# A second-pass down-projection by seven products, LayerNorm tiles turned by DMA, and moved modulation sums

## The chip, the cores and the metric

The kernel runs on one core of one Trainium2 chip. The metric is the device time of one execution in microseconds. The engines are named as in the profile: PE (TensorE matmul), PEld (its weight loads), DVE (VectorE), ACT (ScalarE), POOL (GpSimd), SP (SyncE, which issues most transfers).

## What is computed

The reference is one block: adaptive LayerNorm, attention over a cache, and a gated feed-forward part. x is 2048 x 512, there are 32 query heads of 128 over the last 512 cached keys, and the inner width F is 1792.

```python
mod = (_silu(c) @ w_mod).reshape(c.shape[0], 6, 1, -1)
sa, ca, ga, sb, cb, gb = (mod[:, 0], mod[:, 1], mod[:, 2], mod[:, 3], mod[:, 4], mod[:, 5])
h = _layernorm(x, axis=-1) * (1 + ca) + sa
x = x + ga * _A_ref(h, A_k_cache, A_v_cache, A_wq, A_wo)
h = _layernorm(x, axis=-1) * (1 + cb) + sb
x = x + gb * _B_ref(h, B_w_gate, B_w_up, B_w_down)   # (gelu(h @ w_gate) * (h @ w_up)) @ w_down
```

## The kernel before, in words

**Arithmetic.** Each f32 operand is split into two f16 halves, a high and a low one ("pair"), and a product is three f16 matmuls (`mm3`, lines 85 to 88: low x high, high x low, high x high). A matmul has 128 rows of contraction, a 128 x 128 stationary tile and 512 moving columns.

**Stages.** First the modulation vectors and the first LayerNorm; then attention in 512 steps t of one 128-row score tile each (`scores`, `peak`, `expo`, `recips`, `high`, `low`); then the feed-forward part. Attention runs in two halves of 1024 rows (t up to 255, and from 256). The rows' running sum lies in eight tiles `acc`. When a half's last head is done, `attn_final` stores the tile; in the first half it also normalises it for the feed-forward part (`ln_tile` with gen 2), in the second it only keeps the statistics (`ln_last`).

**Feed-forward.** Rows are taken in two passes of 1024 (two blocks of 512, qb 0 and 1), F in seven pairs of 128-wide tiles. n = 0 to 13 counts pairs over both passes; a round q = 2n + m computes the gate (m = 0) or the up-projection (m = 1) of a pair for both row blocks. Each round uses Strassen's scheme in its seven-product form on blocks of 2 x 2: products 1 to 7 (`PROD`, `CHAIN`, order in `ORDER`) of six matmuls each. They build up in three PSUM banks: chain `a` (products 1, 6, 7, 4; ACT copies the partial sum out after 1, 6 and 7: `keep`, L847), `b` (2) and `c` (5, 3). DVE adds the copies and banks (L1232); ACT and DVE apply the gelu (L1239, L1242, L1245, L1249); in m = 1 DVE multiplies gate and up (L1260), ACT makes the f16 high part (L1262) and DVE the low part (L1263). The results are the four tiles A["11"], A["21"], A["12"], A["22"]: columns of the pair by block of rows.

**Down-projection.** `y_tasks` multiplies A with two 128 x 512 tiles of w_down (`WO["f", n, 0 or 1]`): per pair eight row tiles of two groups of three matmuls, each with its own bank `py`, and DVE adds the bank to `acc` (L914). The eight tasks of a pair wait in `nexty`; `y_next` takes one after each of four of the seven products of a round, so that PE has something between products of one chain.

**What sets the order.** In attention the order on every engine is written out by hand (`tc.manual_schedule`, positions t in `at`, `sched`). In the feed-forward part a planner orders the engines' instructions by program order and readiness, with its own estimate of times; only SP keeps the order in which its transfers are written, and a transfer that waits holds up all behind it. `f_at(q, k, ...)` hangs work on the place behind the k-th product of round q; a "step" is 7q + k.

**Other work around the change.** Gate and up weights come as pairs from DRAM (`set_fetch`, on SP), the combined input blocks of the second pass ("gen 3") are made in the first: `ln_tile(3, i)` loads a row tile, normalises it on ACT (L487), turns it with four f32 transposes on PE (L495, bank `pln`), applies scale and shift on ACT in four 128-wide passes (L503), and spills it; `combos(3, p)` reads the spilled tiles back into `raw` buffers and makes differences on POOL (L540, L367). Tile pools limit how much is in flight: `raw` 5 buffers, `rw` 2, `p16` 4, `pt` 3, PSUM `acc` 5 banks, `s` 2, `qa` 1. The modulation sums for shift and scale (j = 3, 4) are eight products with a running sum on DVE (`mod_col`, L135) at steps t = 211 to 229 of attention; `mod_scale` at t = 234 scales them.

Of the kernel before, what the change touches and what calls it, by code (L numbers as in the profile page):

```python
# [10 lines left out]
F32 = mybir.dt.float32  # L11
# [6 lines left out]
P = 128  # L18
# [45 lines left out]
def block_kernel(ctx: ExitStack, tc: tile.TileContext, x, kT, v, wq, wo, wg, wu, wd, cT, wc, wm, out):  # L64
# [248 lines left out]

    def store(key, t, slack=6):
# [150 lines left out]
    def ln_tile(gen, i, src):  # L465
# [11 lines left out]
        def stat():  # L477
            ln_stat(st["x"], st)
            ln_power(st)
            if gen == 2:  # L480
                st["nm"] = small.tile([P, 1], F32, name="nmean")
                pool_ts(st["nm"], st["mv"][:, 0:1], st["rs"], -1.0)

        def norm():
            if gen == 3:
                rs, nm = col("kmax", qb * QT + i), col("kinv", qb * QT + i)
                return nc.scalar.activation(st["x"], st["x"], AF.Identity, bias=nm, scale=rs)  # L487
            if gen == 2:
                return nc.scalar.activation(st["x"], st["x"], AF.Identity, bias=st["nm"], scale=st["rs"])
            nc.vector.tensor_scalar(st["x"], st["x"], st["mv"][:, 0:1], st["rs"], op0=ALU.subtract, op1=ALU.mult)  # L490
# [6 lines left out]
        def affine(dts):  # L497
# [7 lines left out]
            if KT - 1 in dts:  # L505
                def spill():
                    dma(spilled(gen, qb)[:, :, i * P:(i + 1) * P], f.rearrange("p (k q) -> p k q", k=KT))

                if gen == 3:
                    put_off(3, spill)  # L510
                else:
                    spill()

# [10 lines left out]

        more = [lambda: parts(True), lambda: parts(False)] if gen < 3 else []
        return load, [nop if gen == 3 else stat, norm, turn, lambda: affine((0, 1)), lambda: affine((2, 3))] + more

# [308 lines left out]
    def banks(st, tags):  # L836
        def bk(k):
            def get():
                if k not in st:
                    st[k] = bank(*tags[k])  # L840
                return st[k]
            return get
        return bk
# [289 lines left out]
    at(("w", 232), lambda: mx.update(m=mod_max(3)))  # L1133
    at(234, lambda: mod_scale(3, "mf", 1.0, mx["m"]))

# [79 lines left out]
    NQ = 4 * NP  # L1215
    B, A, G = {}, {}, {}

# [8 lines left out]
    def f_items(q, hold=None):  # L1226
# [27 lines left out]
        def result(key, src):  # L1254
# [3 lines left out]
            else:  # L1258
                g = G.pop((n, key))
                nc.vector.scalar_tensor_tensor(g, g, 0.5 * GU, src, op0=ALU.mult, op1=ALU.mult)  # L1260
                t = pair("ot", "at", NOT)
                nc.scalar.activation(t[:, 0, :], g, AF.Copy)  # L1262
                nc.vector.tensor_tensor(t[:, 1, :], g, t[:, 0, :], op=ALU.subtract)  # L1263
                A[n, key] = t

# [27 lines left out]

        tags = {"a": ("s", "fa", 2) if q else ("qa", "fa", 1), "b": ("acc", "fb", NACC), "c": ("acc", "fc", NACC)}
        return with_posts(("f", q), 2 + q // (2 * NP), banks(st, tags), after)

    def f_spread_at(q):
# [224 lines left out]


    def y_next():
        if nexty:
            all_of(nexty.pop(0))
    ORDER = (1, 2, 6, 7, 5, 4, 3)

    def f_at(q, k, *fns):
        at(("f", q, k), *fns)  # L1530

    for n in range(1, 2 * NP):
        for k in range(2):
            f_at(2 * n + 1, 2 * k, lambda n=n, k=k: WO.update({("f", n, k): fetch(("wd", n % NP, k), get_wo())}))
    for q in range(3, NQ):
        for k, at_ in ((0, 2), (3, 2), (1, 3), (2, 4)):
            f_at(q - 1, at_, lambda q=q, k=k: set_fetch(("f", q), ("f", q % (2 * NP)), k))

    for i in range(2 * QT):
        load, steps = ln_tile(3, i, lambda i=i: y1[2 * QT + i])  # L1540
        q = 7 * (2 + i // 2) + 3 * (i % 2)
        f_at((q - 4) // 7, (q - 4) % 7, load)
        for k, fn in zip((0, 2, 4, 5, 6), steps):
            f_at((q + k) // 7, (q + k) % 7, fn)
    for p in range(2):
        q = 7 * (7 + 2 * p)
        for load, steps in combos(3, p, nc.gpsimd):
            f_at((q - 2) // 7, (q - 2) % 7, load)
            for off, fn in steps:
                f_at((q + 2 * off) // 7, (q + 2 * off) % 7, fn)  # L1550

# [8 lines left out]
    for q in range(NQ):  # L1560
        n, m = divmod(q, 2)
        its = items(NG + q) if q < 2 else f_items(q)
        for k, pk in enumerate(ORDER):
# [11 lines left out]
    while nexty:  # L1575
        y_next()
    while waits_:
        tick()
# [35 lines left out]
```

## Time and profile before

| what | us |
|---|---|
| three runs | 1769.34, 1772.45, 1772.27; median 1772.27 |
| the profiled execution | 1769.1 |
| its span | 1767.3 |
| PE busy | 1730.0 (98%) |
| DVE busy | 1447.2 (82%) |
| ACT busy | 1219.3 (69%) |
| POOL busy | 882.2 (50%) |

The feed-forward part begins at about 1345 us of the span. A group's row reads: line, engine, operation, output <- inputs, shapes, count, then busy time in all and the mean of one in ns, then the idle time of the engine just before and what ended it. A window's row reads: stretch, length, then busy time of PE, PEld, DVE, ACT and POOL with counts, granted PE clock, DMA share, GB/s. A row of waits reads: who waited for whom, us in all, times, longest.

### The profile page before, as it was taken

The page shows a single profiled execution, that of the slowest core. Times are in us where ns is not written, and L with a number is a line of the kernel's source. Part 1 is how long each engine was busy: PE and PEld are TensorE (multiplying, and loading weights), DVE is VectorE, ACT ScalarE, POOL GpSimd, SP SyncE. Part 2 cuts the span into 40 slices and gives each one's busy share as a digit, 9 for nine tenths or more (in the row PEclk, how much of TensorE's full clock was granted, in tenths as well). Part 3 has the DMA queues.
Part 4 walks back from the last instruction along what each step waited for, and adds up shares of the span by engine and source line. Part 5 has one row for each costly group of instructions (what it writes and reads, how often), then busy time and mean ns, then how long its engine had stood idle before and what let it go on. Part 6 is the DMA issues. An engine that isn't in the chain of part 4 may idle for free.

```text
span 1767.3 us, 25992 instructions
## 1 busy us (share of the span) xinstructions
PE 1730.0 (98%) x8114; PEld 796.3 (45%) x8114; DVE 1447.2 (82%) x2501; ACT 1219.3 (69%) x2830; POOL 882.2 (50%) x1119
## 2 busy tenths in 40 slices
PE   7899999999999999999999999999999999999998
PEld 4444444444444444444444444444444444444443
DVE  7888888888888998888888888888886768767676
ACT  5887787878778777897777777777674555434342
POOL 4879878776788873444565555555520024000000
PEclk9999999999999999999999999999999999999999
DMA  7999999989999997999999999999985643252222
GB/s 230 209 195 210 218 217 200 223 204 221 216 216 227 224 201 145 208 205 234 208 208 208 212 214 204 206 211 214 188 185 131 199 129 114 83 173 90 86 75 75
DMA packets 662122, 327.62 MB, mean 185 GB/s; under 512 B 553056, under 2 KB 575840, under 8 KB 661984
## 3 DMA queue, kind: packets, MB, share of 16 engines
q1 hardware_dynamic: 661696, 325.44, 80.0%
q8 instruction: 64, 1.05, 0.3%
q14 instruction: 74, 0.61, 0.1%
q10 hardware_dynamic: 288, 0.52, 0.1%
HBM read 131.73 MB, written 59.90 MB: 108 GB/s over the span
## 4 chain that ended last, share of the span: by engine, by line
PE 72%; DVE 14%; ACT 8%; issue 3%; POOL 2%; DMA 1%; SPq 0%; ACTq 0%; POOLq 0%; DVEq 0%
PE py L86 7%; PE py L88 7%; PE py L87 7%; DVE p L971 5%; PE ps L86 4%; PE ps L88 4%; PE ps L87 4%; PE po L86 4%; PE po L88 4%; PE po L87 4%; DVE nm L945 3%; PE fa L86 3%; PE fa L88 3%; PE fa L87 3%; ACT ee L954 2%
## 5 line engine op out<-in xcount | busy, mean ns | idle before, releaser
L954 ACT ACTIVATE ee<-ps,nm 128x512 f32<-128x512 f32 x512 | 350.9, 685 | 251.0 <-DVE nm L945 245.6
L971 DVE SCALAR_TENSOR_TENSOR p<-ee,rr,p 128x512 f16<-128x512 f32 x512 | 470.0, 918 | 0.9 <-ACT p L966 0.7
L945 DVE TENSOR_REDUCE nm<-ps 128x1 f32<-128x512 f32 x512 | 349.4, 683 | 77.0 <-PE ps L88 75.5
L966 ACT ACTIVATE p<-ee,rr 128x512 f16<-128x512 f32 x512 | 365.4, 714 | 2.3 <-DMA pt<-p 1.9
L86 PE MATMUL ps<-k,qt 128*128 128x512 f16 x512 | 194.1, 379 | 16.6 <-DVE qt L706 15.4
L86 PE MATMUL py<-wo,ot 128*128 128x512 f16 x512 | 194.1, 379 | 4.4 <-DVE ot L706 4.4
L87 PE MATMUL po<-pt,v 128*128 128x512 f16 x512 | 194.0, 379 | 0.0
L88 PE MATMUL po<-pt,v 128*128 128x512 f16 x512 | 194.0, 379 | 0.0
L87 PE MATMUL py<-wo,ot 128*128 128x512 f16 x512 | 194.0, 379 | 0.0
L88 PE MATMUL py<-wo,ot 128*128 128x512 f16 x512 | 194.0, 379 | 0.0
L86 PE MATMUL po<-pt,v 128*128 128x512 f16 x512 | 194.0, 379 | 0.0
L88 PE MATMUL ps<-k,qt 128*128 128x512 f16 x512 | 194.0, 379 | 0.0
L87 PE MATMUL ps<-k,qt 128*128 128x512 f16 x512 | 193.9, 379 | 0.0
L962 DVE RECIPROCAL rr<-rr 128x2 f32<-128x2 f32 x256 | 41.4, 162 | 99.6 <-ACT rr L959 98.5
L87 PEld LDWEIGHTS <-w 128*128 128x128 f16 x728 | 71.2, 98 | 86.2 <-issue 1.2
L88 PEld LDWEIGHTS <-w 128*128 128x128 f16 x728 | 71.2, 98 | 86.0 <-issue 0.2
L86 PEld LDWEIGHTS <-w 128*128 128x128 f16 x728 | 71.2, 98 | 85.5 <-DVE w L1016 0.3
L914 DVE SCALAR_TENSOR_TENSOR acc<-py,dysc,acc 128x512 f32<-128x512 f32 x112 | 81.6, 747 | 31.5 <-PE py L88 30.5
L954 ACT ACTIVATION_READ_ACCUMULATOR ee<-ps,nm 128x1 f32 x512 | 100.8, 197 | 0.0
L914 DVE SCALAR_TENSOR_TENSOR acc<-py,ysc,acc 128x512 f32<-128x512 f32 x128 | 94.7, 740 | 3.9 <-PE py L88 3.9
L706 DVE SCALAR_TENSOR_TENSOR ot<-po,ot 128x512 f16<-128x512 f32 x128 | 87.0, 680 | 0.0
L86 PE MATMUL py<-wo,at 128*128 128x512 f16 x224 | 84.9, 379 | 1.4 <-DVE at L1263 1.4
(270 smaller groups left out, 3765.9 us busy)
## 6 DMA issues: line engine op xcount, KB each, us to landing
w<-kept SPq DMA_DIRECT2D x123, 256.0 KB, 3.2
wo<-kept SPq DMA_DIRECT2D x60, 256.0 KB, 3.5
raw<-in_wo SPq DMA_DIRECT2D x56, 256.0 KB, 3.1
kept<-stage SPq DMA_DIRECT2D x56, 256.0 KB, 3.3
kept<-w SPq DMA_DIRECT2D x39, 256.0 KB, 3.4
rw<-in_wq SPq DMA_DIRECT2D x38, 256.0 KB, 3.3
hs<-hf SPq DMA_DIRECT2D x32, 256.0 KB, 2.7
pt<-p SPq DMA_TRANSPOSE x512, 3.5
```

The lines of the kernel that those rows point to most:

```text
L86: nc.tensor.matmul(ps, llo, rhi, start=first, stop=False, skip_group_check=chain)
L87: nc.tensor.matmul(ps, lhi, rlo, start=False, stop=False, skip_group_check=chain)
L88: nc.tensor.matmul(ps, lhi, rhi, start=False, stop=last, skip_group_check=chain)
L706: return lambda: nc.vector.scalar_tensor_tensor(t[:, 1, :], src, scale, t[:, 0, :], op0=ALU.mult, op1=ALU.subtract)
L914: nc.vector.scalar_tensor_tensor(acc[ti], st["p"], by, acc[ti], op0=ALU.mult, op1=ALU.add)
L945: nc.vector.tensor_reduce(nm, E[t]["ps"], axis=AX.X, op=ALU.max, negate=True)
L954: nc.scalar.activation(e, E[t]["ps"], AF.Exp, bias=E[t]["nm"], scale=1.0, accum_out=sm[:, t % 2:t % 2 + 1])
L962: return lambda: nc.vector.reciprocal(r, r)
L966: nc.scalar.activation(p16[:, 0, :], E[t]["e"], AF.Copy, scale=E[t]["r"])
L971: nc.vector.scalar_tensor_tensor(p16[:, 1, :], E[t]["e"], E[t]["r"], p16[:, 0, :], op0=ALU.mult, op1=ALU.subtract)
```

## The change

- For the pairs n = 7 to 12 (`seven(n)`, all of the second pass but its last) the down-projection is done by seven products too. Four combined activation tiles "s1" to "s4" are built by POOL (`y_sums`: four sums or differences of 128 x 512 f32, then per tile an ACT copy to f16 and a POOL difference). `y_seven` runs two times seven products; each is six matmuls with 256 moving columns, so 84 of 256 take the place of 48 of 512. Chain "a" of it is copied out by ACT after products 1, 6 and 7, scaled, and POOL adds it in two 256-wide pieces to `acc`; after 2, 5, 3 and 4 DVE adds the bank to `acc` in two 256-wide pieces (`defer`red behind the next entry). The steps begin four products into the round after the pair, one after each of the seven products.
- The combined w_down tiles are made in the first pass by POOL (`wd_combined`), which also issues their loads and stores; four instead of two w_down tiles are fetched for those pairs.
- `chain_tag`: chain "a" of rounds and of `y_seven` rotates over three banks (`qa` and the two `s`).
- The eight gen-3 tiles are split into f16 high and low by ACT and POOL and turned by a transposing DMA on SP (`ln_turned`); scale and shift are applied to four turned tiles at once by ACT and DVE (`turned_out`).
- The gen-2 normalisation goes from ACT to POOL. The modulation sums move from t = 211 to 229 to t = 243 to 257, the scaling from 232/234 to 258/260. `combos(3, p)` starts two steps later.
- In the last round `y_next` runs after products k = 1 to 5.

```diff
     def store(key, t, slack=6, eng=None):
...
-            dma(KEPT[key], t)
+            (eng.dma_start if eng else dma)(KEPT[key], t)
...
         def norm():
             if gen == 2:
-                return nc.scalar.activation(st["x"], st["x"], AF.Identity, bias=st["nm"], scale=st["rs"])
+                return pool_ts(st["x"], st["x"], st["mv"][:, 0:1], st["rs"], ALU.subtract, ALU.mult)
...
+    def ln_turned(i):
...
+        def norm():
+            nc.scalar.activation(st["x"], st["x"], AF.Identity, bias=col("kinv", i), scale=col("kmax", i))
+
+        def split():
+            st["p"] = t = pool.tile([P, 2, W], F16, tag="p16", name="xh", bufs=NP16)
+            nc.scalar.activation(t[:, 0, :], st["x"], AF.Copy)
+            nc.gpsimd.tensor_tensor(t[:, 1, :], st["x"], t[:, 0, :], op=ALU.subtract)
+
+        def turn():
...
+            nc.sync.dma_start_transpose(TURN[qb][:, i_], st["p"].rearrange("p a b -> p (a b)"))
...
+    def turned_out(qb, dt):
+        f = tmp("hf")
+        v = f.rearrange("p (t q) -> p t q", t=QT)
+        sc = cols[:, 4, dt:dt + 1]
+        nc.scalar.activation(v, TURN[qb][:, :, dt, :], AF.Identity, scale=sc, bias=cols[:, 3, dt:dt + 1])
+        nc.vector.scalar_tensor_tensor(v, TURN[qb][:, :, KT + dt, :], sc, v, op0=ALU.mult, op1=ALU.add)
+        put_off(3, lambda: dma(spilled(3, qb)[:, dt, :], f))
...
-    for j, ts_ in ((3, (211, 215, 223, 227)), (4, (213, 217, 225, 229)), (5, (274, 278, 282, 286))):
+    for j, ts_ in ((3, (243, 247, 251, 255)), (4, (245, 249, 253, 257)), (5, (274, 278, 282, 286))):
...
+    def y_sums(n):
+        g11, g21, g12, g22 = (R.pop((n, k)) for k in ("11", "21", "12", "22"))
+        nc.gpsimd.tensor_tensor(g22, g12, g22, op=ALU.add)
+        nc.gpsimd.tensor_tensor(g12, g11, g12, op=ALU.subtract)
+        nc.gpsimd.tensor_tensor(g11, g22, g11, op=ALU.subtract)
+        nc.gpsimd.tensor_tensor(g21, g21, g11, op=ALU.subtract)
...
+            nc.scalar.activation(t[:, 0, :], src, AF.Copy)
+            nc.gpsimd.tensor_tensor(t[:, 1, :], src, t[:, 0, :], op=ALU.subtract)
+            A[n, f"s{k + 1}"] = t
+
+        for i, (k, src) in enumerate(((0, g22), (1, g11), (3, g21), (2, g12))):
+            at(("f", 2 * n + 2, 1 + i), lambda k=k, src=src: split(k, src))
...
+    def chain_tag():
+        chains[0] += 1
+        return (("qa", "fa", 1), ("s", "fa", 2), ("s", "fa", 2))[(chains[0] - 1) % 3]
...
+    YPROD = {1: ("a", "11", 0, 0, "keep", 0, 0), 2: ("b", "21", 1, 0, "add", 0, 0), 5: ("c", "s1", 2, 0, "add", 1, 1),
+             6: ("a", "s2", 3, 1, "keep", 0, 1), 3: ("c", "s4", 1, 1, "add", 0, 1), 7: ("a", "s3", 2, 1, "keep", 1, 1),
+             4: ("a", "22", 3, 0, "add", 1, 0)}
+
+    def y_seven(n, x):
...
+            for ii in range(2):
+                sl = slice((2 * x + ii) * P, (2 * x + ii + 1) * P)
+                mm3(st[ch][:, 256 * ii:256 * ii + 256], A[n, a][:, 0, sl], A[n, a][:, 1, sl], w[:, 0, rs], w[:, 1, rs],
+                    k in (1, 2, 5) and ii == 0, k in (2, 3, 4) and ii == 1, True)
+
+        def post(k):
...
+            if what == "keep":
+                src = pool.tile([P, 512], F32, tag="rw", name="yk", bufs=NRW)
+                nc.scalar.activation(src, st[ch], AF.Copy, scale=by)
+            for ii in range(2):
+                t = acc[(2 * (n // NP) + qi) * QT + 2 * x + ii][:, 256 * h:256 * h + 256]
+                s_ = src[:, 256 * ii:256 * ii + 256]
+                if what == "keep":
+                    nc.gpsimd.tensor_tensor(t, t, s_, op=ALU.add)
+                else:
+                    defer.append(lambda t=t, s_=s_: nc.vector.scalar_tensor_tensor(t, s_, by, t, op0=ALU.mult, op1=ALU.add))
+
+        return [[(lambda k=k: go(k), None), (nop, lambda k=k: post(k))] for k in (1, 2, 5, 6, 3, 7, 4)]
...
+    def wd_combined(n, q):
...
+            nc.gpsimd.dma_start(st[k], wd[(2 * n + k) * P:(2 * n + k + 1) * P, :])
...
+    for n in range(NP - 1):
+        wd_combined(n, 2 * n + 3)
...
-            if k in (1, 2, 5, 6):
+            if n > NP and q < NQ - 1 or k in ((1, 2, 5, 6) if q < NQ - 1 else (1, 2, 3, 4, 5)):
                 y_next()
-        if m == 1:
+        if m == 1 and seven(n):
+            f_at(q + 1, 4, lambda n=n: nexty.extend(y_seven(n, 0) + y_seven(n, 1)))
+        elif m == 1:
```

More of the change, by code (lines that the diff above doesn't have):

```diff
@@ L505, in affine @@
             if KT - 1 in dts:
[L506 to L512, printed above, removed]
+                dma(spilled(gen, qb)[:, :, i * P:(i + 1) * P], f.rearrange("p (k q) -> p k q", k=KT))
         def parts(act):
@@ L1259, in result @@
                 g = G.pop((n, key))
[L1260 to L1264, printed above, removed]
+                dst = src if seven(n) and key != "21" else get_qt32() if seven(n) else g
+                nc.vector.scalar_tensor_tensor(dst, g, 0.5 * GU, src, op0=ALU.mult, op1=ALU.mult)
+                R[n, key] = dst
+                if not seven(n) or key != "12":
+                    t = pair("ot", "at", NOT)
+                    nc.scalar.activation(t[:, 0, :], dst, AF.Copy)
+                    nc.vector.tensor_tensor(t[:, 1, :], dst, t[:, 0, :], op=ALU.subtract)
+                    A[n, key] = t
+                if seven(n) and key == "12":
+                    y_sums(n)
         def out_(key, src):
@@ L1532, in block_kernel @@
+    for n in range(NP - 1):
+        wd_combined(n, 2 * n + 3)
     for n in range(1, 2 * NP):
-        for k in range(2):
-            f_at(2 * n + 1, 2 * k, lambda n=n, k=k: WO.update({("f", n, k): fetch(("wd", n % NP, k), get_wo())}))
+        for k in range(4 if seven(n) else 2):
+            f_at(2 * n + 1, 1 + k if seven(n) else 2 * k, lambda n=n, k=k: WO.update({("f", n, k): fetch(("wd", n % NP, k), get_wo())}))
     for q in range(3, NQ):
@@ L1576, in block_kernel @@
         y_next()
+    for fn in defer:
+        fn()
     while waits_:
```

100 lines of the change are left out of this document (78 added, 22 removed).

## The prediction

> **What bounds the kernel now.** I read the page first (span, busy shares), then PE's waits in the feed-forward stage, then busy time by window, and last the single rows that carry a price.
>
> ```profile
> span 1767.3 us, 25992 instructions
> PE 1730.0 (98%) x8114; PEld 796.3 (45%) x8114; DVE 1447.2 (82%) x2501; ACT 1219.3 (69%) x2830; POOL 882.2 (50%) x1119
> ```
>
> PE is busy in 98% of the span; since matmuls overlap, I ask next whether it ever waits. From 1345 us to the end (the feed-forward part) the view of PE's waits has two rows:
>
> ```profile
> PE py L86 <- DVE at L1263: 1.4, 1, 1.4
> PE fa L86 <- ACT fg L847: 0.7, 1, 0.7
> ```
>
> That is 2.1 us in 422. There the time is PE's count of matmuls times their spacing. For the spacing I take 78 matmuls without a gap in PE's timeline, the first of them and the one after the last:
>
> ```profile
> 1358.15 0.38 PE L86 MATMUL py<-wo,ot 128*128 128x512 f16 x1
> 1374.99 0.38 PE L86 MATMUL fa<-t,w 128*128 128x512 f16 x1
> ```
>
> 16.84 / 78 = 0.2159 us (the 0.38 is the time of one from start to end, not the spacing). One F-pair n is two rounds q of 42 matmuls and 48 of the down-projection: 132 x 0.2159 = 28.5 us. The windows (PE, PEld, DVE, ACT, POOL, then clock) show the second pass and one attention stretch in which all engines work:
>
> ```profile
> 480.00:520.00 40.00, 40.00 (x191) 18.40 (x189) 34.27 (x64) 32.60 (x82) 31.86 (x37) 1.00 1.09 234
> 1580.00:1740.00 160.00, 160.00 (x743) 72.50 (x741) 111.17 (x170) 64.36 (x102) 0.00 (x0) 1.00 0.28 91
> ```
>
> In the second pass DVE has 31% free, ACT 60%, and POOL does nothing, at full clock. Fewer PE columns there are worth their full time as long as the others follow.
>
> **The down-projection, six pairs (n = 7 to 12).** It removes 48 matmuls of 512 columns, 48 x 0.2159 = 10.36 us a pair, and adds 2 x 7 products x 6 = 84 of 256 columns. No f16 matmul of 256 columns stands in the trace. The nearest rows are four f32 transposes of 128 columns (as many bytes a row as 256 in f16), each with a weight load of its own, and the loads:
>
> ```profile
> 1385.35 0.60 PE L495 MATMUL pln<-ident,xs 128*128 128x128 f32 x4
> 1385.78 0.38 PE L86 MATMUL fa<-b,w 128*128 128x512 f16 x1
> L495 PEld LDWEIGHTS pln<-ident,xs 128*128 128x128 f32 x32 | 4.0, 141 | 1.5
> L87 PEld LDWEIGHTS <-at 128*128 128x128 f16 x224 | 21.9, 98 | 26.0
> ```
>
> They follow each other at 0.43 / 4 = 0.1075 us although each load takes 0.141; the f16 load takes only 0.098. Low end: half of 0.2159, 84 x 0.108 = 9.07 us. High end: a fixed part per matmul, the line through 128 columns at 0.1075 and 512 at 0.2159, gives 0.1436 at 256: 12.06 us. I take 0.109, next to the row with equal bytes and a longer load: 9.16 us, so 1.2 us a pair and **-7.2 us** in six (ends -7.7 and +10.2).
>
> The Trainium skill, "TensorE: Matmul & The Clock Gate", section "Back-to-back issue gap", speaks against the change: in a stream of load and matmul the pitch is set by both, about 81 ns at 128 columns and 131 ns at 512. An estimate from that page of the Trainium skill for 256 is 98 ns: 8.2 us against 6.3, a loss of 11.5 us in six pairs. This trace's 0.2159 us at 512 does not agree with its 131 ns.
>
> What must follow PE in the new pair of 27.3 us (84 x 0.2159 + 9.16), from these rows:
>
> ```profile
> L914 DVE SCALAR_TENSOR_TENSOR acc<-py,dysc,acc 128x512 f32<-128x512 f32 x112 | 81.6, 747 | 31.5 <-PE py L88 30.5 <-DMA wo<-kept 0.3
> L183 DVE TENSOR_SCALAR lw<-pst 128x1 f32<-128x1 f32 x37 | 7.9, 214 | 0.6 <-PE pst L220 0.6
> L1232 DVE TENSOR_TENSOR u<-u,fc 128x512 f32<-128x512 f32 x28 | 19.1, 683 | 17.2 <-ACT u L847 12.8 <-PE fc L88 4.4
> L1260 DVE SCALAR_TENSOR_TENSOR fg<-fg,u 128x512 f32<-128x512 f32 x28 | 19.2, 687 | 0.4
> L1262 ACT ACTIVATE at<-fg 128x512 f16<-128x512 f32 x56 | 35.1, 626 | 55.6 <-DVE fg L1260 55.6
> L847 ACT ACTIVATE fg<-fa 128x512 f32<-128x512 f32 x39 | 23.0, 591 | 50.6 <-PE fa L88 50.5
> L540 POOL TENSOR_TENSOR cb<-cb x27: 1257/1269/1779, 102.5 to 1484.4; 128x512 f32<-128x512 f32 x27
> L367 POOL TENSOR_TENSOR b<-cb,b 128x512 f16<-128x512 f32 x6 | 6.9, 1154 | 80.9 <-ACT b L363 80.9
> L760 POOL TENSOR_TENSOR rw<-rw x64: 722/727/1282, 128.6 to 741.5; 128x256 f32<-128x256 f32 x64
> ```
>
> DVE: eight adds of 512 become 16 of 256, estimated at 0.48 each (0.214 for almost no columns, half of the rest of 0.747): 7.7 us; six sums 4.1 and 15 products and differences at 0.687, 10.3. Together 22.1 us. ACT: 11.5 us now (64.36 us over 5.6 pairs), plus three splits and six copies, 16.9. POOL: four sums 5.1, four differences 4.6, 12 adds of 256 at 0.727, 8.7: 18.4 us. All stay below 27.3, and in the window from 480 us DVE at 86% and POOL at 80% left PE without a gap.
>
> What POOL costs DVE shows in the softmax product, which like 12 of DVE's operations here reads two SBUF tiles (the columns are shortest, median, longest ns):
>
> ```profile
> L971 DVE SCALAR_TENSOR_TENSOR p<-ee,rr,p x512: 723/743/1809, 36.9 to 1343.9; 128x512 f16<-128x512 f32 x171
> L971 DVE SCALAR_TENSOR_TENSOR p<-ee,rr,p 128x512 f16<-128x512 f32 x512 | 470.0, 918 | 0.9 <-ACT p L966 0.7
> ```
>
> Mean 0.918 against a median of 0.743: 0.175 each, 2.1 us a pair, DVE 24.2 us. Still below.
>
> The Trainium skill, "SBUF — State Buffer", section "Who interferes with whom", says that a Vector operation with two SBUF inputs and a GpSimd one that reads SBUF lock each other out for a whole instruction. The longest row, 1.809, agrees; the mean shows how seldom it is that bad.
>
> Order: the first combined tile needs, after the round's last product, DVE 1.4, four sums 5.1, four adds queued between 2.9, ACT 0.63, POOL 1.15: 11.2 us. PE has until then seven products (9.1) and seven down-projection steps (4.6), 13.7 us. On time by 2.5; late by about 2.2 if every POOL operation took its longest time (+4.7). The copies on ACT wait for two `rw` tiles that POOL frees; behind them on ACT stand copies for which PE's chain waits. I put **+2.0 us** for all new waits of both passes, ends 0 and 15 (2.5 x 6), near the low one because of the 2.1 us above.
>
> **First pass.** These rows price it (the last two are windows, POOL's busy time the fifth figure):
>
> ```profile
> L503 ACT ACTIVATE hf<-pln,cols 128x128 f32<-128x128 f32 x96 | 37.8, 463 | 1.2 <-DMA hs<-hf 1.2
> L156 POOL TENSOR_SCALAR stage<-raw 128x512 f16<-128x512 f32 x14 | 12.3, 881 | 1.3
> L1369 POOL TENSOR_TENSOR raw<-raw,gs 128x512 f32<-128x512 f32 x14 | 18.6, 1331 | 0.6
> L157 POOL TENSOR_TENSOR stage<-raw,stage 128x512 f16<-128x512 f32 x14 | 17.3, 1238 | 1.2
> 1360.00:1460.00 100.00, 100.00 (x481) 47.48 (x479) 68.11 (x110) 50.28 (x95) 18.05 (x30) 1.00 0.51 160
> 1460.00:1555.00 95.00, 95.00 (x442) 43.04 (x440) 70.92 (x106) 42.72 (x69) 17.89 (x14) 1.00 0.28 91
> ```
>
> Gone are 32 transposes, 32 x 0.1075 = **-3.4 us**, and ACT's four passes of 0.46 a tile, for which ACT gets a copy a tile and eight shared passes: no more work than before. POOL combines weights in 6 x 10.7 us (a scaling 0.88, two products 2.66, four differences 2.9, two splits 4.24) and takes over eight differences of the tiles (10 us); it also issues 24 transfers, of which no row exists: from nothing up to 3.5 us each they fit, since of the 195 us 36 are busy and 74 are added. So that hides; without this cover the second pass would wait for its weights. Eight transposing transfers enter SP's queue and wait for POOL; behind them stand the weight loads. What such a block costs today:
>
> ```profile
> SPq L94 <- ACT hf L503: 18.4, 2, 16.5
> ```
>
> SP stood 16.5 us in one wait and PE lost nothing. The new weight tiles take two of five `raw` buffers while four gen-3 tiles are loaded twice; a fourth load blocked until POOL frees one would delay a weight load, at most about 4 us each time: in the 0 to 15 above.
>
> **Tail.** Six steps (6 x 6 x 0.109 = 3.9 us) now lie behind the last product and cover the 1.4 us wait for `at` in the first fence of waits: **-1.4**.
>
> **Modulation sums and the gen-2 normalisation.** Eight sums on DVE leave 569-620 us for about 655-695 (from the first to the last, steps 211 to 229, it took 49.6 us, 2.75 a step).
>
> ```profile
> 569.03 1.64 DVE L135 SCALAR_TENSOR_TENSOR wmc<-wmc,sbc 128x512 f32<-128x512 f32 x1
> 618.59 0.68 DVE L135 SCALAR_TENSOR_TENSOR wmc<-wmc,sbc 128x512 f32<-128x512 f32 x1
> L135 DVE DVE_READ_ACCUMULATOR wmc<-wmc,sbc x12: 76/77/84, 570.6 to 768.9; 128x1 f32 x12
> L135 DVE SCALAR_TENSOR_TENSOR wmc<-wmc,sbc x12: 676/683/1642, 569.0 to 768.3; 128x512 f32<-128x512 f32 x12
> 560.00:580.00 20.00, 19.03 (x90) 8.36 (x89) 17.56 (x36) 16.27 (x43) 17.56 (x23) 1.00 1.06 241
> 600.00:620.00 20.00, 17.67 (x83) 7.70 (x81) 19.25 (x38) 13.31 (x32) 16.49 (x24) 1.00 0.83 204
> 660.00:680.00 20.00, 20.00 (x94) 9.10 (x93) 18.15 (x31) 15.35 (x38) 9.10 (x10) 1.00 0.78 158
> 680.00:700.00 20.00, 20.00 (x94) 9.11 (x93) 15.66 (x30) 13.73 (x33) 6.95 (x9) 1.00 0.72 138
> 700.00:720.00 20.00, 20.00 (x97) 9.27 (x96) 19.29 (x35) 16.35 (x39) 5.47 (x8) 1.00 0.97 197
> ```
>
> PE misses 0.97 and 2.33 us where they are. Where they go, DVE has 1.85 + 4.34 = 6.2 us free and they need 8 x 0.76 = 6.1. I take a gain of half the 3.3, **-1.5**, ends -4 and +4; in the +4 is the scaling behind them, which lands in 700-720, where DVE has 0.7 free. The normalisation moves from ACT to POOL, 5.5 of 20 us busy there: nothing; without that cover, a step's delay.
>
> **Sum.** -7.2 - 3.4 + 2.0 - 1.4 - 1.5 = -11.5 us. The profiled execution took 1769.1 us (span 1767.3): 1757.6. The median shown, 1772.27, is 3.2 higher; the same sum gives **1760.8 us**.
>
> **Rivals.** *Late tiles:* PE stands for POOL's combined tiles or a delayed weight load. For it: six chains of 11 us on the slowest engine; against: the 2.5 us of room and the windows at 80%. With 6 to 15 us instead of 2.0: 1765 to 1774. *A fixed part per matmul (slower):* at 0.1436 the six pairs cost +10.2 in place of -7.2, 1778; it turns to a loss where the spacing passes 0.132 (4.3 us of other gains over six pairs, 11.08 / 84). For it: no row of that shape; against: the transposes, whose loads are longer. By the figures of the Trainium skill's page on TensorE the same mechanism gives 1779.5. *DVE held by POOL (slower):* 22.1 + 12 waits; above 0.43 us each DVE passes 27.3, above 0.6 the kernel is slower, and at the longest, 1.07, it would be near 1806; against: the mean of 0.175. *All ends good:* -7.7 - 3.4 - 1.4 - 4, no new waits: 1755.8.
>
> **Chances.** Forecast, 1757 to 1766: 0.58. All ends good, 1752 to 1757: 0.12. Late tiles: 0.17, of it 0.07 below 1768.7. Fixed part: 0.08. DVE held: 0.05. A measurement here can tell 0.2%, 3.5 us, from no change: faster 0.77, same 0.10, slower 0.13. The range 1752 to 1774 leaves out both slower cases and little else.
>
> **What would show it.** The spacing of the 256-column `py` matmuls (0.109 or 0.14); PE's waits from 1345 us on (below 3 us, or rows of several us on `as` tiles, on ACT's `yk` copies or on weight transfers); no `pln` matmul after 1345; no gap at the last product; PE in 560-720 us. I am wrong if PE's waits there grow by more than 10 us, or if DVE is above 95% in the second pass.

## The result, and the profile after

The changed kernel took 1782.67 us (median of 6 runs, 1780.82 to 1786.74), the kernel before 1772.36 beside it on the same chip: ratio 1.0061, 95% interval 1.0049 to 1.0074. By the ratio it is slower by about 10.8 us; the prediction was 11.5 us faster. The profiled execution took 1782.8 us, its span 1781.0. In the new kernel line numbers have moved: L869 is the old L847 (ACT copies a bank), L1280 the old L1232 (DVE adds bank and copy), L936 the old L914, L1309, L1313, L1314 the old L1260, L1262, L1263.

The page, span and busy times:

```profile
span 1781.0 us, 26800 instructions
PE 1728.9 (97%) x8298; PEld 814.9 (46%) x8298; DVE 1496.6 (84%) x2551; ACT 1243.0 (70%) x2860; POOL 1104.3 (62%) x1337
```

TensorE's busy time hardly fell: a matmul counts as busy to its end, 0.38 us after its start, and so does a slow stretch that is shown below. The waits of PE from 1345 us to the end say more (who waited for whom, us in all, times, longest):

```profile
PE fa L86 <- ACT u L869: 4.1, 3, 1.8
PE py L86 <- DVE fg L1280: 4.1, 1, 4.1
PE fa L86 <- ACT fg L869: 3.8, 6, 1.0
PE fa L86 <- DMA w<-kept: 2.8, 2, 1.8
PE fc L86 <- DVE u L1280: 2.4, 1, 2.4
PE py L86 <- DVE acc L936: 1.3, 1, 1.3
...
PE py L86 <- POOL as L1260: 0.8, 2, 0.5
PE py L86 <- DVE at L1314: 0.8, 1, 0.8
```

All ten rows of this view (two are left out) add up to 21.7 us, where before there were 2.1. They name ACT, DVE, a transfer and POOL: no single engine. By window (PE, PEld, DVE, ACT, POOL, then clock):

```profile
560.00:580.00 20.00, 19.32 (x91) 8.61 (x90) 16.18 (x32) 16.93 (x43) 15.76 (x23) 1.00 0.99 225
600.00:620.00 20.00, 19.90 (x95) 8.89 (x93) 16.02 (x32) 13.87 (x34) 18.24 (x28) 1.00 0.85 208
1360.00:1460.00 100.00, 92.77 (x427) 41.59 (x426) 82.69 (x113) 44.99 (x72) 58.40 (x72) 1.00 0.66 192
1460.00:1555.00 95.00, 87.38 (x391) 38.62 (x390) 79.08 (x93) 41.78 (x70) 66.41 (x65) 0.96 0.41 134
1580.00:1740.00 160.00, 155.49 (x925) 90.04 (x923) 123.23 (x202) 88.38 (x145) 101.04 (x99) 1.00 0.42 134
```

In the two attention windows PE now misses 0.8 us where it missed 3.3. In the first pass it misses 14.8 of 195 us where it missed none, with a mean granted clock of 0.96 in its second window; in the second pass it misses 4.5 of 160. So the loss is mostly in the first pass, which the change gives no matmul to. The second pass has its fewer columns, at the spacing that I took; PE's timeline:

```profile
1627.30 0.27 PE L86 MATMUL fa<-wo,at 128*128 128x256 f16 x1
...
1627.85 0.27 PE L88 MATMUL fa<-wo,at 128*128 128x256 f16 x1
1629.03 0.38 PE L86 MATMUL fa<-t,w 128*128 128x512 f16 x1 [0.91 <-ACT fg L869]
```

Five steps in 0.55 us: 0.11 each.

**The largest gap.** PE's, DVE's and POOL's timeline of the changed kernel in the first pass (start, duration, what it waited for in brackets):

```profile
1495.09 0.39 PE L86 MATMUL fa<-b,w 128*128 128x512 f16 x1 [1.77 <-DMA w<-kept]
...
1501.59 0.59 PE L86 MATMUL py<-wo,at 128*128 128x512 f16 x1 [4.07 <-DVE fg L1280]
1501.97 0.63 PE L87 MATMUL py<-wo,at 128*128 128x512 f16 x1
...
1507.33 0.38 PE L86 MATMUL py<-wo,at 128*128 128x512 f16 x1
1494.98 5.36 DVE L1314 TENSOR_TENSOR at<-fg,at 128x512 f16<-128x512 f32 x1 [2.83 <-ACT at L1313]
1494.42 1.16 POOL L157 TENSOR_TENSOR wdc<-raw,wdc 128x512 f16<-128x512 f32 x1
...
1497.76 1.25 POOL L562 TENSOR_TENSOR cb<-cb 128x512 f32<-128x512 f32 x1
1498.96 0.56 POOL L320 DMA_DIRECT2D kept<-wdc  x1
...
1500.09 1.26 POOL L367 TENSOR_TENSOR t<-cb,t 128x512 f16<-128x512 f32 x1
```

One DVE subtraction of two SBUF tiles, 0.69 us when alone, lasted 5.36 us, while POOL ran four instructions (L157, L367 twice, L562) without a break; DVE was done at 1500.34, 0.25 us after POOL had issued two transfers (1498.96 to 1500.09). DVE's next sum was late and PE stood for 4.1 us. Behind the gap PE's matmuls come up to 0.43 us apart instead of 0.216, 14 of them from 1501.59 to 1507.33 us: 2.7 us more. The granted clock of that stretch is 0.52. This looked like the rival "DVE held by POOL", and I took it as the theory. Against it stood a second one, from ACT's timeline:

```profile
1427.52 0.81 ACT L528 ACTIVATE xs<-xs,kinv,kmax 128x512 f32<-128x512 f32 x1 [2.72 <-DMA xs<-y]
...
1432.24 0.57 ACT L869 ACTIVATE u<-fa 128x512 f32<-128x512 f32 x1
```

ACT stood 2.7 us for a LayerNorm tile's load, and behind it in its order stood the bank copy for which PE waited 1.6 us. That tile lies in one of the five `raw` buffers, of which the combined weights now take two. For this instance the trace shows another cause, though: its load was issued at 1422.65 us, and just before SP had stood 7.0 us for the spill of a turned tile that DVE had to finish (first row below). A wait for a `raw` buffer shows in the two rows behind it:

```profile
SPq L94 <- DVE hf L547: 7.0, 1, 7.0
...
1475.72 14.56 SPq L94 DMA_DIRECT2D cb<-hs  x4
SPq L94 <- POOL wdc L157: 8.5, 1, 8.5
```

SP's four loads into `raw` buffers took from 1475.72 to 1490.3 to issue, 8.5 us of it for POOL's `wdc`; the weight tiles behind them made the 1.77 us wait of PE at 1495. So the rivals were: DVE held by POOL's arithmetic, or transfers held by the shared buffers.

### The profile page after: what moved, and what is told of

It reads as the page before. It is cut to its first block, busy times and chain, and to the rows that moved or that the text cites. A ratio compares the mean times of both kernels' runs of the same rounds, so it can differ in the third digit from the quotient of the medians.

```text
span 1781.0 us, 26800 instructions
## 1 busy us (share of the span) xinstructions
PE 1728.9 (97%) x8298; PEld 814.9 (46%) x8298; DVE 1496.6 (84%) x2551; ACT 1243.0 (70%) x2860; POOL 1104.3 (62%) x1337
## 4 chain that ended last, share of the span: by engine, by line
PE 58%; DVE 18%; ACT 8%; POOL 6%; issue 5%; DMA 3%; SPq 1%; DVEq 0%; POOLq 0%; ACTq 0%
PE py L86 5%; PE py L87 5%; PE py L88 5%; DVE p L993 5%; PE ps L86 4%; PE ps L88 4%; PE ps L87 4%; PE po L86 4%; PE po L88 4%; PE po L87 4%; DVE nm L967 3%; ACT ee L976 2%; ACT p L988 2%; PE qa L86 2%; PE qa L88 2%
## 5 line engine op out<-in xcount | busy, mean ns | idle before, releaser
L936 DVE SCALAR_TENSOR_TENSOR acc<-py,ysc,acc 128x512 f32<-128x512 f32 x128 | 94.7, 740 | 3.7 <-PE py L88 3.7
L386 POOL TENSOR_TENSOR rs<-rs,nhalf 128x1 f32<-128x1 f32 x32 | 18.8, 589 | 119.9 <-DVE rs L380 117.3
L233 POOL TENSOR_TENSOR lw<-lw,half__86 128x1 f32<-128x1 f32 x37 | 21.5, 581 | 111.5 <-DVE lw L183 111.4
L1624 POOL TENSOR_TENSOR acc<-acc,yk 128x256 f32<-128x256 f32 x72 | 60.8, 868 | 46.9 <-ACT yk L1619 46.9
```

What stands on the lines that cost most here:

```text
L233: nc.gpsimd.tensor_tensor(out, out, half_, op=ALU.pow)
L386: nc.gpsimd.tensor_tensor(st["rs"], st["rs"], nhalf, op=ALU.pow)
L936: nc.vector.scalar_tensor_tensor(acc[ti], st["p"], by, acc[ti], op0=ALU.mult, op1=ALU.add)
L1624: nc.gpsimd.tensor_tensor(t, t, s_, op=ALU.add)
```

## The experiments

All times are medians; a ratio is to the kernel before on the same chip, with its 95% interval. Differences between runs of different calls are taken between ratios (0.1% is 1.77 us).

**A ladder of parts.** e1 is the kernel before with two edits, shown in part (the scaling moves to t = 258 and 260 as well; the sums move by 28 to 32 steps, not by 32 to 40 as the text below says):

```diff
-    for j, ts_ in ((3, (211, 215, 223, 227)), (4, (213, 217, 225, 229)), ...
+    for j, ts_ in ((3, (243, 247, 251, 255)), (4, (245, 249, 253, 257)), ...
-                return nc.scalar.activation(st["x"], st["x"], AF.Identity, bias=st["nm"], scale=st["rs"])
+                return pool_ts(st["x"], st["x"], st["mv"][:, 0:1], st["rs"], ALU.subtract, ALU.mult)
```

> The kernel before with two parts of the change alone: the modulation sums 32 to 40 steps later, and the second LayerNorm's normalisation on GpSimd. In the changed kernel the same event (the wait of fa for fg at the start of the feed-forward part) comes at 1352.23 where it was at 1355.57, 3.3 us earlier. If this gain belongs to these two edits, the time is 3.3 us under before, 1769 (1768 to 1770). The rival, that the gain comes from the banks and buffers that the other parts change, gives 1772.

e2 is the changed kernel less the products and the combined weights (and with `y_next` behind products 1, 2, 5 and 6 again):

```diff
-        return NP <= n < 2 * NP - 1
+        return False
...
-    for n in range(NP - 1):
-        wd_combined(n, 2 * n + 3)
```

> The changed kernel without the seven products of the second down-projection and without the combined tiles of w_down on GpSimd: what is left is the attention part's edits, the LayerNorm tiles turned by DMA, and the third bank of the chain. Theory (GpSimd's work on the combined tiles holds VectorE): pass 1 has few gaps, 32 transposes are gone (3.4 us), so 1769 less 3.4, 1766 (1763 to 1769). Rival (the turned tiles themselves, with their 1.4 us additions on VectorE, make the chain late): pass 1 keeps most of its 19 us, 1778 or more.

e3 keeps the products, and drops only the last two lines, with `k % 2` for `k` in the fetch of w_down:

> The changed kernel without the work on the combined tiles of w_down: the seven products read the two plain tiles in their place (so the second pass multiplies by other weights), and pass 1 has none of the loads, scalings, subtractions, splits and stores. Theory: the 19 us of TensorE gaps of pass 1 go, with them the slow clock behind the 4 us gap, and the 8.4 us of pass 2 stay: 1782.7 less 16 to 19, 1764 to 1767. Rival (the turned tiles or the combinations' loads make pass 1 late): 1778 or more.

Measured: e1 1765.08 us, 0.9965 (0.9953 to 0.9978); e2 1763.96, 0.9962 (0.9950 to 0.9975); e3 1767.19, 0.9975 (0.9964 to 0.9986). In steps of ratios: attention -6.2 us, turned tiles -0.5, seven products +2.3, combined weights +15.2. e1 gained more than either side had expected. An interval is about 2 us to each side, so the two small steps are not clear of noise. The first pass's loss is the combined weights', the turned tiles are about even, and no gain of the seven products is seen even without them.

**Arithmetic on another engine (e4).**

```diff
-            nc.gpsimd.tensor_tensor(o, a, c, op=ALU.subtract)
+            nc.vector.tensor_tensor(o, a, c, op=ALU.subtract)
```

and so for the scaling, the gate and the splits (their copies on ACT).

> The changed kernel with the elementwise work on the combined tiles moved from GpSimd to VectorE and ScalarE: two scalings of 512, four subtractions of 256 and two of 512 per pair on VectorE, two copies on ScalarE, the loads and stores left on GpSimd's queue. VectorE gets about 4.5 us more work per pair in a part in which it is busy for 83 of 100 us. Theory (VectorE is held while GpSimd runs, for whole rows of its instructions): the single instruction of 5.4 us goes, pass 1 loses at most half of its 19 us, 1768 to 1775. Rival (the work as such is too much, or the load buffers it holds make the weights late): pass 1 loses as much or more, 1781 to 1795.

1784.32 us, 1.0072 (1.0059 to 1.0084): as the rival said. The theory of DVE held by POOL's combined work was in trouble, but the work now loads DVE itself and holds the shared buffers as before, so this run alone does not decide.

**Moves without arithmetic, and own buffers (e5, e6).** e5 leaves out `gate`, `scaled` and `combine`, ACT writes both halves. e6 changes one line:

```diff
-            st[k] = raw("raw")
+            st[k] = pool.tile([P, 512], F32, tag="rw", name="rwd", bufs=NRW)
```

> The changed kernel with the combined tiles' arithmetic left out: GpSimd's queue still issues the loads of w_down and the stores, ScalarE writes the two halves of each tile as plain copies (so the second pass multiplies by other weights), and GpSimd computes nothing for them. It holds the load buffers as long as before. Theory (GpSimd's arithmetic is what makes pass 1 late): no more than 3 us over the kernel without the combined work (1767.2), 1767 to 1770. Rival (the buffers held, the loads and the issues on GpSimd's queue make the weights late): most of the 15.5 us stay, 1777 to 1783.

> The changed kernel with one size changed: the raw tiles of w_down lie in two buffers of their own (those of the attention part's weight loads, idle in pass 1) and no longer in the five that the combinations' loads and the LayerNorm tiles rotate through. All arithmetic stays. Theory (GpSimd's arithmetic holds VectorE): the wait of 1.8 us for a weight tile goes and little else, 1779 to 1783. Rival (SyncE's queue is blocked by the buffers): most of the 15.5 us go, 1767 to 1772.

e5: 1772.92, 1.0011 (1.0003 to 1.0020), 6.4 us over e3. e6: 1769.85, 1.0001 (0.9991 to 1.0010), 4.6 over e3 and 10.6 under the changed kernel. Both predictions of the theory failed, and e5 also missed the rival's range: with all of POOL's arithmetic in place, two buffers of its own take away two thirds of the 15.2 us. Without the arithmetic (6.4) or without the sharing (4.6) the work costs far less than with both. The 6.4 us are no price of held buffers: in e5's first pass PE's one long wait, 5.4 us for a weight tile, stands behind a spill of a turned tile for which SP waited 11.4 us.

That DVE is still stretched on average without this loss is seen in the groups of DVE's instructions between 1380 and 1515 us, first with own buffers, then without the combined work (e3):

```profile
L1314 DVE TENSOR_TENSOR at<-fg,at 128x512 f16<-128x512 f32 x18 | 19.8, 1100 | 2.9 <-ACT at L1313 2.4
```
```profile
L1314 DVE TENSOR_TENSOR at<-fg,at 128x512 f16<-128x512 f32 x19 | 14.1, 741 | 3.7 <-ACT at L1313 3.2
```

A mean of 1.10 us against 0.74, and the time differs by 4.6 us in all. With own buffers no DVE instruction from 1370 us on lasted over 2.1 us. Single rows as long as the 5.4 us of the changed kernel come back in e9 and e16 below.

**Memsets (e7).** Each POOL operation on the combined weights becomes `nc.gpsimd.memset` of the same tile.

> The changed kernel with each of GpSimd's operations on the combined tiles replaced by a memset of the same tile (the products read zeros): GpSimd writes as much and reads nothing. Theory (VectorE and GpSimd keep each other off while both read from SBUF): VectorE is no longer stretched by these, 1767 to 1772. Rival (GpSimd is too busy as such, the combinations and splits queued behind come late): as far as the memsets last as long as what they replace, most of the loss stays, 1776 to 1783.

1768.21 us, 0.9988 (0.9979 to 0.9996). In the theory's range, but it does not tell reading from load, since the memsets were far shorter than what they replaced (POOL's groups: first the memsets, then the changed kernel's differences):

```profile
L1649 POOL MEMSET raw<- 128x256 f32 x24 | 6.6, 317 | 0.0
```
```profile
L1649 POOL TENSOR_TENSOR raw<-raw 128x256 f32<-128x256 f32 x24 | 20.8, 868 | 0.2
```

It agrees with the buffer theory, too: buffers held for a shorter time.

**Combined weights in attention (e8).** `prep_wd` makes them from the tiles it has scaled anyway, and `wd_combined` is gone (the main lines):

```diff
+        if n < NP - 1:
+            more_ = [staged() for _ in range(2)]
...
+            sched(b + 1, (lambda: load(1), [lambda: stat(1), spread, nop, combine, nop]), b + 4, b + 9, b + 10, b + 13)
```

> The changed kernel with the combined tiles of w_down made in the attention part, right behind the plain ones and from the same loads and scalings: 12 loads and 12 scalings fewer, the four subtractions and two splits per pair moved to where TensorE is busy 99% of the time and GpSimd 50%. The output is the reference's. Theory: the feed-forward part takes what it takes without the combined work, and the attention part has room for 6 times about 6 us of GpSimd: 1765 to 1769. Rival (the DMA engines, busy 0.94 to 1.01 in that part, or VectorE, busy 85%, have no room): 1772 to 1780.

1779.29, 1.0048 (1.0035 to 1.0062): the rival's side. In its profile the wait of `fa` at the start of the feed-forward part comes 11 us later than in the changed kernel (1363.44 against 1352.23), and the feed-forward part itself is as short as in e3. Whether DMA or DVE was short of room in attention was not tried.

**Buffers or order (e9 to e12).** In the feed-forward part the planner writes another order of instructions after any edit, so e6 could have been lucky. Two pairs: the work three products later, with shared and own buffers; and the program's own order on every engine (the edits, the second one in part),

```diff
-            f_at(q + d // 7, d % 7, fn)
+            f_at(q + (d + 3) // 7, (d + 3) % 7, fn)
```
```diff
+    with tc.manual_schedule():
...
+        for q in range(NQ):
```

> The changed kernel with the combined tiles' work three steps (products) later; the load buffers stay shared. In the feed-forward part a planner orders the engines' instructions, so each edit there also gives another order. Theory (a load that waits for a shared buffer holds all transfers behind it): about as slow as the changed kernel, 1777 to 1786. Rival (the changed kernel is slow by the order that the planner happened to choose, and own buffers were quick by theirs): the time may land anywhere, below 1774 as likely as not.

> The same shift by three steps with the two buffers of its own for the raw tiles of w_down. Theory (shared buffers): near the unshifted kernel with own buffers, 1767 to 1773, and at least 6 us under the shifted kernel with shared ones. Rival (the planner's order): no fixed difference from the shifted kernel with shared buffers.

> The changed kernel with every engine's instructions of the feed-forward part in the order in which the program writes them, no longer in the planner's; buffers shared. Together with the next run it holds the order fixed and changes the buffers alone. Where this order as such puts the time is open: 1765 to 1800.

> The program's own order again, with two buffers of their own for the raw tiles of w_down: all engines' instructions and SyncE's transfers stand in the same order as in the run before, only buffers differ. Theory (the shared buffers cost the time): 8 to 13 us under the run before. Rival (the gain of own buffers was one of order): within 2 us of it.

e9: 1785.98, 1.0086 (1.0072 to 1.0099). e10: 1771.30, 1.0002 (0.9993 to 1.0011). e11: 1883.99, 1.0636 (1.0616 to 1.0655). e12: 1872.50, 1.0573 (1.0558 to 1.0587). Own buffers give 14.7 us in the shifted pair and 11.5 at a fixed order. So the loss hangs on the sharing of the `raw` buffers, in three orders; and in the planner's order the four versions with own buffers (e6, e10, and e15 and e16 below) lie from 1769.4 to 1771.5, the two with shared ones at 1782.7 and 1786.0. Whether two more buffers in the shared ring would do as well as a ring of their own was not tried. The program's order as such is 100 us worse than the planner's, far outside the range expected for e11.

At the fixed order one can see where. PE's waits between 1480 and 1620 us, SP's for `wdc` there, SP's loads and PE's first matmul behind them, shared buffers:

```profile
PE fa L86 <- DMA w<-kept: 10.8, 2, 7.4
...
SPq L94 <- POOL wdc L157: 21.2, 2, 14.3
1508.93 16.87 SPq L94 DMA_DIRECT2D cb<-hs  x4
...
1526.37 0.38 SPq L94 DMA_DIRECT2D w<-kept  x1
1530.74 0.61 PE L86 MATMUL fa<-b,w 128*128 128x512 f16 x1 [7.40 <-DMA w<-kept]
```

and with own buffers, where neither a wait for `w<-kept` on PE nor one for `wdc` on SP is left:

```profile
PE fa L86 <- ACT fg L869: 9.7, 6, 3.5
...
1501.64 11.46 SPq L94 DMA_DIRECT2D cb<-hs  x3
...
1513.67 0.38 SPq L94 DMA_DIRECT2D w<-kept  x1
```

The gate weight is issued 12.7 us earlier. The chain reads: POOL's `wdc` frees a `raw` buffer late, SP's combination load waits for it, the weight tiles behind that load are late, PE stands. SP also waits for POOL's `t` there, with own buffers as well (27.7 and 25.7 us); what own buffers take away is the 21.2 us for `wdc`.

In the planner's order this chain shows only in small part (8.5 us of SP and 1.77 us of PE in the changed kernel). The largest waits there stand behind single long DVE rows. In e9 one lasted 8.09 us beside six POOL instructions; ACT stood 7.1 us for DVE's next result with PE's bank copy behind it. Another lasted 4.22 us:

```profile
1488.49 8.09 DVE L1297 SCALAR_TENSOR_TENSOR fg<-sq,fg 128x512 f32<-128x512 f32 x1 [0.74 <-ACT sq L1293]
...
1499.12 0.58 PE L86 MATMUL fa<-t,w 128*128 128x512 f16 x1 [7.86 <-ACT u L869]
...
1519.65 0.61 PE L86 MATMUL py<-wo,at 128*128 128x512 f16 x1 [3.52 <-DVE at L1314]
```

Behind both waits 14 matmuls come slowly again. In the feed-forward part, DVE instructions of over 2.7 us stand in the changed kernel, e4 and e9, and with own buffers in e16 (4.60 us). Without the combined weights none there is over 1.8 us, and at the fixed order none over 2.1 us, with shared buffers (e11) or own ones (e12). So "DVE held by POOL" is a part of the path in the planner's order, beside the queue. It does not follow from POOL's work without a break alone: in e6 POOL was busy for all of 1459 to 1494 us, and no DVE instruction there lasted over 1.8 us. What brings the long rows, and how much of the 10.6 us each path takes, is open.

**The attention part (e13, e14).** e1's two edits apart, the sums (with their scaling) and the normalisation.

> The kernel before with the modulation sums and their scaling 24 to 32 steps later, and nothing else. The two edits of the attention part together gave 6.3 us. If they belong to the sums (eight products of VectorE out of 569 to 620 us, where TensorE missed 3.3 us), the time is 4 to 6.5 us under before, 1764.5 to 1767; if to the normalisation, within 1.5 us of before.

> The kernel before with the second LayerNorm's normalisation on GpSimd in place of ScalarE, and nothing else. If the gain belongs to the sums: within 1.5 us of before, 1769.5 to 1772.5. If ScalarE's relief counts: 2 to 6 us under before.

e13: 1764.00, 0.9964 (0.9952 to 0.9977). e14: 1770.90, 1.0002 (0.9993 to 1.0011). As far as the intervals tell, all of it is the sums'. Windows before that the prediction does not show, then e13's:

```profile
620.00:640.00 20.00, 19.36 (x91) 8.70 (x90) 18.80 (x37) 13.44 (x31) 15.58 (x16) 1.00 0.97 200
640.00:660.00 20.00, 18.25 (x86) 8.10 (x85) 17.10 (x27) 15.36 (x37) 14.33 (x14) 1.00 0.90 196
```
```profile
600.00:620.00 20.00, 19.89 (x94) 8.93 (x93) 16.12 (x31) 13.64 (x34) 18.24 (x28) 1.00 0.83 210
620.00:640.00 20.00, 20.00 (x94) 9.07 (x93) 18.56 (x30) 15.29 (x37) 15.43 (x15) 1.00 0.98 200
640.00:660.00 20.00, 19.37 (x91) 8.62 (x89) 17.61 (x30) 14.82 (x35) 15.39 (x16) 1.00 0.92 206
660.00:680.00 20.00, 20.00 (x95) 9.00 (x94) 19.93 (x40) 13.72 (x34) 6.22 (x6) 1.00 0.92 205
```

PE gains in the two windows behind the sums as well, and where they land DVE is full (19.93 of 20) and PE misses nothing.

**The second pass (e15, e16, e18) and the spills (e16, e17).** e15 is e6 with the steps of the seven products in twos:

```diff
+                for _ in range((2, 0, 2, 2, 0, 1, 0)[k]):
+                    y_next()
```

e16 adds a later spill, which e17 adds to e2:

```diff
-        put_off(3, lambda: dma(spilled(3, qb)[:, dt, :], f))
+        put_off(3 if qb else 6, lambda: dma(spilled(3, qb)[:, dt, :], f))
```

e18 is e3 without `y_sums`: plain tiles stand for "s1" to "s4".

> The changed kernel with own buffers for the raw tiles of w_down, and in the second pass the steps of the seven products taken in twos: two behind products 1, 6 and 7, one behind 4, none behind 2, 5 and 3. Theory for the 7 us of gaps in the second pass: between two products of chain a stands one step of 0.65 us where a down-projection task of 1.3 us stood, and ScalarE's copy of the bank, with copies of yk and as ahead of it, is not done; with 1.3 us again the gaps before fa go, 4 to 6 us under the own buffers alone (1769.9): 1764 to 1766. Rival (the late tiles of GpSimd and ScalarE's load set the gaps, wherever the steps stand): 1768 to 1772.

> The run before with one more edit: the first row block's four turned tiles are written to memory six products after VectorE makes them in place of three, so that SyncE's queue does not stand at them with weight tiles behind (27.7 us of its waits, and 3.6 us of TensorE's for a weight tile, with own buffers). If these spills hold the weights: 2 to 4 us under the run before. If not: within 1.5 us of it.

> What the runs point to as the quicker parts together: the attention part's edits and the turned LayerNorm tiles (1764.0 together), with the first row block's spills six products behind in place of three, and neither the seven products of the second pass nor the combined tiles. If the spills hold the weight tiles (2.1 us of TensorE's gaps in that kernel): 1761 to 1763. If moving them only moves the wait: 1763 to 1765.

> The kernel without the combined work (1767.2), and in the second pass also without GpSimd's sums and the splits of the combined activation tiles: the products read plain tiles in their place, so the output is another; the 256-column matmuls, the copies yk, GpSimd's additions to acc and VectorE's 256-wide ones stay. If the late combined tiles and the load of making them (GpSimd, ScalarE) ate the 7.2 us: 1760 to 1763. If the additions in pieces and the copies yk did: 1765 to 1768.

e15: 1771.54, 1.0006 (0.9997 to 1.0015), no gain over e6: the short cover between products of chain a is not the cause. e16: 1769.39, 0.9995 (0.9987 to 1.0004), 2 us under e15, with intervals that overlap: the spills do hold weights. Its profile has no wait for `w<-kept` from 1345 to 1545 us where e15's had 3.8, but a new one of 3.8 us for ACT's copy, which stood behind the DVE row of 4.60 us. e17: 1764.94, 0.9967 (0.9955 to 0.9979): no better than e2. PE's waits from 1345 us on are 3.8 us (4.8 in e2), 2.3 of them in a new one for DVE. e18: 1759.55, 0.9942 (0.9930 to 0.9955), 5.8 us under e3: most of the lost gain goes into the making of the combined activation tiles, not into the additions in pieces. PE's waits from 1545 us on and the second pass's window, e3 first, then e18:

```profile
PE fa L86 <- ACT fg L869: 2.7, 4, 1.0
PE fa L86 <- DMA w<-kept: 1.9, 1, 1.9
PE py L86 <- POOL as L1260: 0.8, 2, 0.5
...
1580.00:1740.00 160.00, 153.65 (x930) 90.39 (x928) 123.17 (x200) 91.34 (x150) 113.27 (x110) 1.00 0.33 106
```
```profile
PE fa L86 <- DMA w<-kept: 1.3, 1, 1.3
PE fa L86 <- ACT yk L1604: 0.2, 1, 0.2
1580.00:1740.00 160.00, 158.61 (x978) 95.41 (x977) 119.77 (x213) 83.97 (x133) 58.38 (x68) 1.00 0.33 105
```

POOL's work halves, ACT's falls by 7 us, and its bank copies are on time: the rows for ACT `fg` and POOL `as` are gone. Whether POOL's lateness or ACT's splits weigh more is left open. Of the versions that leave nothing out, the quickest are e13 and e2 at 1764 us, 0.36 to 0.38% under before.

## Why the prediction was wrong, by its steps

- **Six pairs, -7.2:** the spacing was right (0.11 us), the rivals with a fixed part per matmul are out, and so is the loss worked out from the Trainium skill, "TensorE: Matmul & The Clock Gate", section "Back-to-back issue gap": 0.216 us at 512 columns and 0.11 at 256 do not agree with its pitch of 131 ns at 512. But the time is saved only if the tiles are there; with them made, the part comes to +2.3 us (e3 against e2), without their making to -3.5 (e18 against e2), or to -5.8 if one compares the two profiled executions from `fa`'s first wait to the end (412.2 and 406.4 us).
- **New waits, +2.0 (0 to 15): the step that failed.** From the total of +10.8 the attention's measured -6.2 (e1) and the -3.4 and -7.2 for fewer matmuls leave +27.6 us for the waits and the end, where +2.0 and -1.4 were put. PE's wait rows grew by 19.6 us (2.1 to 21.7). A row counts from the end of the matmul before, 0.38 us after its start, where the next would have come after 0.216; so each of 18 new waits costs 0.16 more, 3.0 in all. The slow clock behind the largest gap took 2.7, and the end grew by 1.6: together 26.9. The blocked fourth load was named and put at "at most about 4 us each time", counting the one weight load behind it. What it left out: the two combined tiles hold their buffers for as long as POOL takes for its whole queue; single DVE instructions stand for 4 to 8 us beside POOL in the first pass; ACT too works in order, and stands for a late tile or a late DVE result with the bank copies of PE's chain behind it; and a gap of 4 us cost another 2.7 us of slow clock. That the sharing of buffers decides it is shown (10.6, 14.7 and 11.5 us); what brings the long DVE rows stays open. "Against" it I set the room that POOL has on average (36 + 74 of 195 us); that says nothing of how long one buffer is held. The sign that was named for being wrong, PE's waits grown by more than 10 us, is the one that came.
- **"So that hides", of POOL's combined weights:** wrong as written, 15.2 us, right in part with own buffers (4.6 us, the arithmetic).
- **DVE held by POOL:** its bound, 1.07 us an operation, was the longest row of attention and no bound: 5.36 us here, 8.09 in e9. It was priced for the second pass alone; in the first, single long rows carry the largest waits, so this rival is part of what happened. As a steady effect it costs little: with own buffers DVE is stretched as much on average, and everything together costs 4.6 us. The Trainium skill, "SBUF — State Buffer", section "Who interferes with whom", has the lock last a whole instruction; the trace shows one DVE instruction standing beside four POOL instructions in a row.
- **Order in the second pass, 2.5 us of room:** PE waited only 0.8 us for `as` tiles; but their making still cost 5.8 us (e18), and with it went the waits for ACT's bank copies, ahead of which ACT has splits and copies. That wait was named ("behind them on ACT stand copies"), and put too low.
- **Transposes, -3.4:** they are gone, but turning by DMA brought new waits (PE's rows from 1345 us add up to 4.8 us in e2, 2.1 before), and e2's gain over e1 is 0.5 us, within noise: the spills wait for DVE on SP's queue (23 us of its waits in e2), with weight tiles behind.
- **Tail, -1.4:** the wait fell from 1.4 to 0.8 us, and the end, from the last matmul's start, grew from 4.2 to 5.8 us (1775.16 to 1781.0), since two of DVE's last additions now queue there: a loss of 1.
- **Modulation sums and normalisation, -1.5 (-4 to +4):** right in sign and mechanism, too small: 6.4 (e13), beyond the end of -4. Only two windows were priced, and then halved; 620 to 660 us missed 2.4 more. The normalisation costs nothing, as said (e14).

## What to carry to other kernels

Work that is "off the path" has two prices: the engine's time, and how long it holds a buffer from a ring that others use in order. Here a ring of its own took most of the loss away. Before choosing a ring, follow a late load through every in-order queue (SP, and ACT or POOL that read it) to what stands behind. After an edit that lets a planner reorder, compare pairs at the same order or with a second shift before naming a cause.

## What the runs showed of the hardware

A VectorE operation on two SBUF tiles stood for 5.36 us (0.69 alone) beside four GpSimd operations in a row, another for 8.09 beside six (e9); the first ended 0.25 us after GpSimd's next two transfer issues, the second during them. After PE had stood for 4.1 us, 14 matmuls came up to 0.43 us apart instead of 0.216, at a granted clock of 0.52. After a gap of 3.55 us (e6) the next ones came at 0.22, after one of 3.65 us (e10) 13 came slowly. 256-column matmuls follow each other at half the spacing of 512 with no fixed part to be seen (0.109 to 0.216 us), each with its weight load beside it. A transfer issued by GpSimd took 0.56 us of its queue.
